# Weight decoding in three stages a unit apart, a split first load of P, and later loads kept behind, in a one-core kernel of packed attention and two mixtures

## The chip, the core and the metric

The kernel runs on one core of a Trainium2 chip, as one program with one launch. The metric is the device time in microseconds (us). The core has five engines that work in their own order: TensorE (PE, matrix products; PEld is its loading of weights), VectorE (DVE), ScalarE (ACT), GpSimd (POOL) and SyncE (SP), which here issues loads only. ScalarE and GpSimd issue a few as well.

## The reference

Batch B = 4, heads H = 8, sequence S = 576, head dimension D = 64, and 32 packed queries. Attention runs twice: the packed queries p over (k, v), and then q over what that gave. Its output is 2304 tokens of width 512, which go through two layers with 2048 hidden units and Mish, and then through another two with ELU.

```python
def sm_attn(qq, kk, vv):
    s = scale * np.matmul(qq, kk.transpose(0, 1, 3, 2))
    s = s - np.max(s, axis=-1, keepdims=True)
    a = np.exp(s)
    a = a / (np.sum(a, axis=-1, keepdims=True) + 1e-09)
    return np.matmul(a, vv)
p_packed = sm_attn(p, k, v)
out = sm_attn(q, p_packed, p_packed)
...
h = x @ w_in
sp = np.where(h > 20.0, h, np.log1p(np.exp(np.minimum(h, 20.0))))
g = h * np.tanh(sp)
y = g @ w_out
...
h = y @ w_in2
g = np.where(h > 0.0, h, alpha * (np.exp(np.minimum(h, 0.0)) - 1.0))
return g @ w_out2
```

q, k, v and p arrive as float32, the four weight matrices as float64.

## The kernel before, in words

**Weights.** Nothing on the chip computes in float64, so a weight tile of 128 x 512 numbers is loaded as 128 x 1024 integers (`load_raw`, L123) and put together into float32 by `decode` (L135): s0, a prelude on ScalarE (L158 in the form for the beginning, `exps`, with Prelu; L160 with Copy after it); s1 to s3, the merge, on VectorE (L165, L173, L178; the `exps` form has no L173); s4, the high half, on ScalarE (L200); s5, the low half, on VectorE (L206). Products are made in three terms, high by high, high by low and low by high. The tiles of the first layer of mixture 1 (w1i) are not split but kept whole in w1v, and GpSimd stores them in DRAM, from where they are loaded again for later batches (w1r).

**Attention and fold.** `attention_steps(b)` gives the steps of one batch: k is turned (kT), scores of P over k (L302), maximum, exponential and sum (L316 to L333), turning, the packed product (L373, L403), whose result is copied to PT (L271); then q is turned, the second scores (L426 for batch 0, L441 for the others) are turned to tokens by rows (L455), and after exponential and norm they come back as A2h and A2l, two halves (L204). `fold(b, c)` multiplies PT into a quarter of w1i (L519) and splits the result into G[b, c]. So the first layer of mixture 1 is one product of G with A2.

**Units.** Mixture 1 runs over 128 units: four batches, two halves of tokens, 16 blocks of 128 hidden units. A unit is `gemm1` (6 products, L550 to L552, first of them the term high by high), `mish` (Mish on ScalarE L559, high half on ScalarE L560, low half on VectorE L561) and, two units later (LAG), `gemm2` (12 products, L578 to L580, which add to an output in PSUM). In batch 0 the order is blocks 0 to 7 for the first half of the tokens, the same for the second, and then 8 to 15. Mixture 2 (L640 to L665) follows with the same kind of loop; its weights are decoded during mixture 1.

**What sets the order.** `startup()` is written out by hand: on TensorE, VectorE, ScalarE and SyncE its instructions are pinned in the order of the list `order`, in which `parts(n, 1, 3)` stands for steps 1 and 3 of the n-th tile. Eight tiles are decoded there. After it, `mixture1` is a loop over units, and the framework's scheduler may move instructions past each other, apart from those that `tc.keep_in_program_order` names: the prelude and the first merging step of a tile. In the loop, `DEC1=[9, 37]` tells how many w1 tiles are to be decoded by which unit; `decode_w1(m)` runs all six steps of a tile one behind the other. Folds 1 to 3 of batch 0 start at the units in `F0`. Batch 1's attention goes one step at a time, and from unit `FAST0` on at a second place of each unit too.

**Loads.** SyncE issues its loads in one order. An issue that would be the ninth under way waits for one that was issued eight places earlier (ScalarE's issues count among these). A raw tile of mixture 1 lies in a buffer of the pool `up`, and its load also waits until the buffer's last user is done.

Of the kernel before, what the change touches and what calls it, by code (L numbers as in the profile page):

```python
# [9 lines left out]
F32 = mybir.dt.float32  # L10
F32R = mybir.dt.float32r
# [7 lines left out]
    DEC1=[9, 37],  # L19
    F0=[3, 12, 17],  # L20
    LEAD=2,
    ATT1=4,
    FAST0=16,
# [18 lines left out]
def kernel(  # L42
# [71 lines left out]
    pT = const.tile([128, B * H // 2, 2, NP], F32, name="pT")  # L114
# [8 lines left out]
    def load_raw(name, r, c):  # L123
        nm = f"raw_{name}{r}_{c}"
        t = slot([128, 1024], I32, nm) if name[1] == "1" else sg.tile([128, 1024], I32, tag="sg", name=nm)
        nc.sync.dma_start(
            out=t, in_=weights[name][r * 128:(r + 1) * 128, c * 1024:(c + 1) * 1024]
        )
        raws[name, r, c] = t
# [5 lines left out]
    def decode(name, r, c, staged=False, exps=False):  # L135
# [3 lines left out]
        t = dp.tile([128, 512], I32, tag="dec", name="dec")  # L139
# [12 lines left out]
        oi = w1v[key][:, r % 2, :].bitcast(I32) if whole else t  # L152
# [29 lines left out]
        def s4():  # L182
            if whole:
                if r % 2 == 1:
                    nc.gpsimd.dma_start(out=w1_dr[c * 2 + r // 2], in_=w1v[key])
            else:
                split_hi(t.bitcast(F32), parts[:, 0] if staged else wt[key][0][:, r % 2, :], 1.0 / WSCALE)
# [103 lines left out]
    def scores1(b, s):  # L291
        d = {}

        def pe():
            ps = pm()
            d["pair"] = last_pair[0]
            for x in range(2):
                for g in (3, 2, 1, 0):
                    kg = kT[b, g].rearrange("p e s -> p (e s)").rearrange("p (j x t) -> p j x t", x=2, t=32)
                    for th in range(2):  # L300
# [3 lines left out]
                            lhsT=pT[r:r + 32, b * 4 + g, x, :],  # L304
# [206 lines left out]
    def fold(b, c):  # L511
# [20 lines left out]
        return [pe, post]  # L532
# [205 lines left out]
    def decode_w1(m):  # L738
        for _ in range(m):
            if w1dec:  # L740
                for f in next_w1():
                    f()

# [4 lines left out]
    DEC1 = P["DEC1"]  # L748

    def startup():  # L750
        pr = slot([128, B * H // 2, D], F32, "pr")
        ps_ = p.rearrange("b (g s) n d -> s n (b g) d", s=2)
        for s in range(2):
            for th in range(2):
                r = 64 * s + 32 * th
                (nc.sync, nc.scalar)[s].dma_start(out=pr[r:r + 32], in_=ps_[s])
# [13 lines left out]
        load_w1(6)  # L770
# [10 lines left out]
        nc.vector.transpose(  # L781
            out=pT.rearrange("p g x k -> p (g x k)"), in_=pr.rearrange("p g d -> p (g d)")
        )
        a1t0, a1t1 = ta
        order = [
            hk[0][0], hk[1][0], hk[2][0], hk[3][0], sc[0][0], sc[1][0], *parts(0, 0), *parts(0, 1, 3, 4, 5),
            sc[0][1], *parts(1, 0), sc[1][1], *parts(1, 1, 3, 4, 5), sc[0][2], a1t0[0], a1t0[1], pk[0][0], a1t1[0], a1t1[1],
            hq[0][0], hq[1][0], sc[1][2], *parts(2, 0), *parts(3, 0), pk[0][1], pk[1][0], hq[2][0], hq[3][0], pk[1][1], pk[0][2],
            *parts(2, 1, 3), pk[1][2], s2[0], *parts(2, 4, 5), *parts(3, 1, 3, 4, 5), f0[0], s2[1], s2[2],
            s2[3], s2[4], *parts(4, 0), f0[1], s2[5], *parts(4, 1, 3), s2[6], *parts(4, 4), s2[7], *parts(4, 5),  # L790
            *parts(5, 0, 1, 3, 4, 5), *parts(6, 0, 1, 3, 4, 5), *parts(7, 0, 1, 3, 4, 5),
        ]
        for o in order:
            o()

# [17 lines left out]
    def mixture1():  # L813
# [28 lines left out]

        tile2 = 2 * (B - 1) * NK + P['T2']
        for c in (3, 2, 1):
            fol.q.appendleft((F0[c - 1], fold(0, c)))
        for i in range(NA + LAG):
# [101 lines left out]
```

## Time and profile before

| | |
|---|---|
| time, median of 3 runs | 829.34 us (828.67 to 830.78) |
| the profiled execution's own time | 830.86 us |
| its span | 829.1 us |
| mean granted TensorE clock | 0.96 |
| busy: TensorE, VectorE, ScalarE, GpSimd | 777.5, 440.1, 346.6, 22.6 us |
| moved by DMA | 96.80 MB |

The rows further down come from that one profiled execution, in microseconds from the start of its span. A timeline row is a run of like instructions of one line: start, length from the first to the last, engine, line, operation, what it writes and reads, how many, and in brackets the idle time of the engine before it and what ended it. The granted clock is a share of TensorE's full speed, 1.00 being 2.4 GHz and 0.50 being 1.2. Busy time is the time in which an engine worked on an instruction; TensorE's products overlap, so the start of one after another tells the pace, not the length of one.

### The profile page before, as it was taken

The numbers are of one execution on the slowest core, as the hardware profiler recorded it, in microseconds if no ns is written. First come the engines' busy times: TensorE is split into PE (matmuls) and PEld (weight loads), VectorE is DVE, ScalarE is ACT, GpSimd is POOL, SyncE is SP. The second block draws the span as 40 slices with busy tenths as digits, with TensorE's granted clock in tenths as the row PEclk, the third lists the DMA queues.
The fourth block names the chain that finished last, engine by engine and source line by source line (L and its number), as shares of the span: only waits on it lengthen the run. The fifth ranks groups of instructions, "written<-read, shape, count | busy, mean of one in ns | idle before, by whom it ended". The sixth has DMA issues, their size and how long they took to land.

```text
span 829.1 us, 13056 instructions
## 1 busy us (share of the span) xinstructions
PE 777.5 (94%) x5212; PEld 671.0 (81%) x5212; DVE 440.1 (53%) x844; ACT 346.6 (42%) x676; POOL 22.6 (3%) x46
## 2 busy tenths in 40 slices
PE   3656898999999999999999999999999999999997
PEld 3344788979989898899998888888888888888886
DVE  3678788675587466772516753513253334342342
ACT  1265774557465655674534432312141223221222
POOL 0000000000101000000000000000000000000000
PEclk7565998999999999999999999999999999999999
DMA  9954377237656656431592310200020001000000
GB/s 273 372 215 158 120 272 220 81 111 222 197 198 244 191 142 233 142 116 51 180 332 79 127 52 26 76 1 1 1 76 14 1 0 51 13 0 1 26 26 26
DMA packets 69181, 96.80 MB, mean 117 GB/s; under 512 B 36096, under 2 KB 44800, under 8 KB 69120
## 3 DMA queue, kind: packets, MB, share of 16 engines
q1 hardware_dynamic: 62176, 77.22, 29.6%
q0 software_dynamic: 4736, 17.30, 5.3%
q10 hardware_dynamic: 2208, 1.44, 0.7%
q8 instruction: 41, 0.67, 0.3%
q14 instruction: 20, 0.16, 0.1%
HBM read 73.92 MB, written 22.02 MB: 116 GB/s over the span
## 4 chain that ended last, share of the span: by engine, by line
PE 85%; DVE 6%; ACT 4%; DMA 3%; issue 1%; SPq 0%; ACTq 0%; DVEq 0%
PE h L640 8%; PE h L641 8%; PE h L642 8%; PE o L663 8%; PE o L664 8%; PE o L665 8%; PE acc L579 7%; PE acc L578 7%; PE acc L580 7%; PE h L550 4%; PE h L551 4%; PE h L552 4%; PE pm L519 1%; DMA raw_w1i<-in_moe_w_in_dram 1%; DMA raw_w2i<-in_moe_w_in_dram 1%
## 5 line engine op out<-in xcount | busy, mean ns | idle before, releaser
L578 PE MATMUL acc<-gh,w1oh 128*128 128x288 f32 x512 | 150.1, 300 | 5.6 <-ACT w1oh L200 3.4
L579 PE MATMUL acc<-gl,w1oh 128*128 128x288 f32 x512 | 152.8, 300 | 0.1
L580 PE MATMUL acc<-gh,w1ol 128*128 128x288 f32 x512 | 152.3, 300 | 0.0
L641 PE MATMUL h<-yl,w2ih 128*128 128x512 f32 (+1 forms) x320 | 117.7, 368 | 0.0
L642 PE MATMUL h<-yh,w2il 128*128 128x512 f32 (+1 forms) x320 | 117.5, 368 | 0.0
L640 PE MATMUL h<-yh,w2ih 128*128 128x512 f32 (+1 forms) x320 | 116.7, 368 | 0.0
L663 PE MATMUL o<-w2oh,gh 128*128 128x512 f32 x288 | 112.4, 390 | 1.1 <-ACT ob L269 0.7
L664 PE MATMUL o<-w2ol,gh 128*128 128x512 f32 x288 | 112.2, 390 | 0.0
L644 ACT ACTIVATE t<-h 128x512 f32<-128x512 f32 (+1 forms) x80 | 42.8, 553 | 165.3 <-PE h L642 157.5
L665 PE MATMUL o<-w2oh,gl 128*128 128x512 f32 x288 | 108.3, 389 | 0.0
L645 DVE TENSOR_SCALAR t<-t 128x512 f32<-128x512 f32 (+1 forms) x80 | 31.7, 399 | 142.3 <-ACT t L644 141.5
L578 PEld LDWEIGHTS acc<-gh,w1oh 128*128 128x128 f32 x512 | 96.9, 192 | 10.1 <-ACT w1oh L200 3.8
L579 PEld LDWEIGHTS acc<-gl,w1oh 128*128 128x128 f32 x512 | 97.7, 191 | 6.5 <-DVE gl L561 3.2
L580 PEld LDWEIGHTS acc<-gh,w1ol 128*128 128x128 f32 x512 | 97.5, 191 | 5.0 <-issue 4.5
L561 DVE TENSOR_TENSOR gl<-t,gh 128x288 fp32r<-128x288 f32 x128 | 57.8, 453 | 77.9 <-ACT gh L560 77.3
L550 PE MATMUL h<-a2h,gh 128*128 128x288 f32 x256 | 78.7, 310 | 14.4 <-ACT a2h L200 10.5
L559 ACT ACTIVATE t<-h 128x288 f32<-128x288 f32 x128 | 52.2, 409 | 81.4 <-PE h L552 80.1
L551 PE MATMUL h<-a2l,gh 128*128 128x288 f32 x256 | 77.8, 304 | 2.9 <-DVE a2l L204 2.9
L200 ACT ACTIVATE gh<-t 128x512 fp32r<-128x512 f32 (+1 forms) x80 | 46.6, 588 | 78.6 <-DVE t L646 49.5
L552 PE MATMUL h<-a2h,gl 128*128 128x288 f32 x256 | 77.1, 303 | 0.0
L204 DVE TENSOR_TENSOR gl<-t,gh 128x512 fp32r<-128x512 f32 (+1 forms) x80 | 50.3, 638 | 41.0 <-ACT gh L200 39.5
L642 PEld LDWEIGHTS h<-yh,w2il 128*128 128x128 f32 x320 | 60.3, 188 | 10.3
(107 smaller groups left out, 1101.5 us busy)
## 6 DMA issues: line engine op xcount, KB each, us to landing
w1r<-w_dr SPq DMA_DIRECT2D x24, 512.0 KB, 6.4
raw_w2i<-in_moe_w_in_dram SPq DMA_DIRECT2D x16, 512.0 KB, 4.4
raw_w1i<-in_moe_w_in_dram SPq DMA_DIRECT2D x16, 512.0 KB, 8.1
raw_w1o<-in_moe_w_out_dram SPq DMA_DIRECT2D x16, 512.0 KB, 8.1
raw_w2o<-in_moe_w_out_dram SPq DMA_DIRECT2D x16, 512.0 KB, 3.7
k<-in_k_dram SPq DMA_DIRECT2D x16, 288.0 KB, 4.6
y_dr<-y POOLq DMA_DIRECT2D x16, 288.0 KB, 2.9
w_dr<-w1v POOLq DMA_DIRECT2D x8, 512.0 KB, 5.1
```

Source lines behind the costliest of these rows:

```text
L550: nc.tensor.matmul(out=hp, lhsT=wh, rhs=xh, start=(kt == 0), stop=False)
L551: nc.tensor.matmul(out=hp, lhsT=wh, rhs=xl, start=False, stop=False)
L552: nc.tensor.matmul(out=hp, lhsT=wl, rhs=xh, start=False, stop=(kt == 1))
L578: nc.tensor.matmul(out=o, lhsT=wh[:, cs], rhs=gh, start=first, stop=False)
L579: nc.tensor.matmul(out=o, lhsT=wh[:, cs], rhs=gl, start=False, stop=False)
L580: nc.tensor.matmul(out=o, lhsT=wl[:, cs], rhs=gh, start=False, stop=last)
L640: nc.tensor.matmul(out=hp, lhsT=wh, rhs=xh, start=(i == 0), stop=False)
L641: nc.tensor.matmul(out=hp, lhsT=wh, rhs=xl, start=False, stop=False)
L642: nc.tensor.matmul(out=hp, lhsT=wl, rhs=xh, start=False, stop=(i == 3))
L663: nc.tensor.matmul(out=o, lhsT=gh[:, ts], rhs=wh, start=(kk == 0), stop=False)
L664: nc.tensor.matmul(out=o, lhsT=gh[:, ts], rhs=wl, start=False, stop=False)
L665: nc.tensor.matmul(out=o, lhsT=gl[:, ts], rhs=wh, start=False, stop=(kk == NK - 1))
```

## The change

- Decoding in stages. In the loop of mixture 1, each unit starts one tile (unit 0: two): load of the next one, and its prelude (s0). Tiles so started stand in `staged`. Of these, each unit merges (s1 to s3) as many as `NDEC=[2, 4, 6]` and then one more per unit ask for, ahead of `gemm1`; the halves (s4, s5) follow behind `mish` of the next unit. `decode_w1` is gone.
- The merge of a w1i tile writes at once into w1v, without the buffer `dec`.
- P is loaded in two pieces: batch 0 (a quarter) as before by SyncE and ScalarE, the other three by GpSimd's queue ahead of the identity matrix; they are turned at the end of `startup` (`turn_p(1)`).
- The raw loads of mixture 2's weights are kept in program order (`keep_in_program_order`), so the scheduler no longer moves them forward.
- `startup`: ten tiles have their prelude in it and six are finished in it (before: eight and eight); the steps of the tiles stand at other places among those of attention; low halves of G[0, 0] are a step of their own (`post_lo`). Two more tiles are asked for ahead.
- `F0` goes from units 3, 12, 17 to 3, 13, 19, and `FAST0` from 16 to 24.

```diff
-    DEC1=[9, 37],
-    F0=[3, 12, 17],
+    NDEC=[2, 4, 6],
+    F0=[3, 13, 19],
...
-    FAST0=16,
+    FAST0=24,
...
-        nc.sync.dma_start(
+        ins = nc.sync.dma_start(
             out=t, in_=weights[name][r * 128:(r + 1) * 128, c * 1024:(c + 1) * 1024]
         )
+        if name[1] == "2":
+            tc.keep_in_program_order(ins)
...
-        oi = w1v[key][:, r % 2, :].bitcast(I32) if whole else t
+        wv = w1v.get(key)
+        oi = wv[:, r % 2, :].bitcast(I32) if whole else dp.tile([128, 512], I32, tag="dec", name="dec")
+        t = oi
...
-        return [pe, post]
+        return [pe, post] if b or c else [pe, post_hi, post_lo]
...
+        pr = [slot([128, n * H // 2, D], F32, f"pr{n}") for n in (1, B - 1)]
...
+                    eng = nc.gpsimd if x else (nc.sync, nc.scalar)[s]
+                    eng.dma_start(out=pr[x][r:r + 32], in_=ps_[s][:, a:a + n, :])
...
-        load_w1(6)
+        load_w1(8)
...
-        dec = [decode(*w1dec.popleft(), exps=True) for _ in range(8)]
+        dec = [decode(*w1dec.popleft(), exps=True) for _ in range(10)]
...
-            hk[0][0], hk[1][0], hk[2][0], hk[3][0], sc[0][0], sc[1][0], *parts(0, 0), *parts(0, 1, 3, 4, 5),
...
+            hk[0][0], hk[1][0], hk[2][0], hk[3][0], sc[0][0], sc[1][0], sc[0][1], sc[1][1], *parts(0, 0), sc[0][2],
+            a1t0[0], a1t0[1], a1t1[0], a1t1[1], *parts(1, 0), pk[0][0], hq[0][0], hq[1][0], sc[1][2], *parts(0, 1, 3, 4),
+            pk[1][0], pk[0][1], hq[2][0], hq[3][0], pk[0][2], pk[1][1], *parts(2, 0), *parts(3, 0), *parts(1, 1, 3, 4),
+            pk[1][2], s2[0], *parts(2, 1, 3, 4), *parts(3, 1, 3, 4), s2[1], s2[2], f0[0], s2[3], s2[4], f0[1],
+            *parts(4, 0), *parts(5, 0), s2[5], f0[2], *parts(6, 0), *parts(7, 0), s2[6], s2[7],
+            *parts(8, 0), *parts(9, 0), *parts(4, 1, 3, 4), *parts(5, 1, 3, 4), *parts(4, 5), *parts(5, 5),
+            lambda: turn_p(1),
         ]
...
+        staged.extend(dec[6:])
...
-            if len(w1seq) - len(w1dec) < DEC1[0] + (i + 1) * DEC1[1] // 32:
-                m = DEC1[0] + (i + 1) * DEC1[1] // 32 - (len(w1seq) - len(w1dec))
-                load_w1(m + LEAD - (len(w1dec) - len(w1load)))
-                decode_w1(m)
+
+            now = []
+            if staged:
+                done = P["NDEC"]
+                n = done[i] if i < len(done) else done[-1] + i + 1 - len(done)
+                while staged and nmerged[0] < n:
+                    now.append(staged.popleft())
+                    nmerged[0] += 1
+            for _ in range(2 if i < 1 else 1):
+                if w1dec:
+                    load_w1(1)
+                    staged.append(next_w1())
+                    staged[-1][0]()
+            for t in now:
+                for f in t[1:4]:
+                    f()
             if i < NA:
                 gemm1(i)
             if i < NA:
                 mish(i)
+            for t in merged:
+                for f in t[4:6]:
+                    f()
+            merged[:] = now
```

How the instructions stand on the engines shows more than the diff, since the scheduler moves some of them. In the rows below a line is one instruction in its engine's order, L is the line of the kernel (lines of the changed kernel lie 1 to 15 further down), and the numbers behind a name tell buffers apart. First SyncE, from the last k of batch 0 on. Before:

```order
L249 DMA k0_3_148<-in_k_dram 128x576
L126 DMA raw_w2i0_1_1924<-in_moe2_w_in_dram 128x1024
L126 DMA raw_w2i1_1_1926<-in_moe2_w_in_dram 128x1024
L126 DMA raw_w1i0_0_163<-in_moe_w_in_dram 128x1024
L126 DMA raw_w1i1_0_165<-in_moe_w_in_dram 128x1024
L249 DMA q0_0_167<-in_q_dram 128x576
L249 DMA q0_1_169<-in_q_dram 128x576
```

After the change:

```order
L253 DMA k0_3_154<-in_k_dram 128x576
L127 DMA raw_w1i0_0_169<-in_moe_w_in_dram 128x1024
L127 DMA raw_w1i1_0_171<-in_moe_w_in_dram 128x1024
L253 DMA q0_0_173<-in_q_dram 128x576
L253 DMA q0_1_175<-in_q_dram 128x576
L253 DMA q0_2_177<-in_q_dram 128x576
L253 DMA q0_3_179<-in_q_dram 128x576
```

The two loads of raw_w2i, mixture 2's weights, are no longer there: the first tiles of mixture 1 (raw_w1i) and q follow k at once.

Second, VectorE right behind the turning of k. Before:

```order
L281 STREAM_TRANSPOSE kT0_3_212<-k0_3_148 128x576
L165 TENSOR_SCALAR dec_191<-raw_w1i0_0_163 128x512
L178 SCALAR_TENSOR_TENSOR w1v0_0_192<-raw_w1i0_0_163,dec_191 128x512
L316 TENSOR_REDUCE sm_251<-pm_214 128x1
L317 TENSOR_SCALAR sm_251<-sm_251 128x1
L316 TENSOR_REDUCE sm_258<-pm_231 128x1
L317 TENSOR_SCALAR sm_258<-sm_258 128x1
L165 TENSOR_SCALAR dec_193<-raw_w1i1_0_165 128x512
L178 SCALAR_TENSOR_TENSOR w1v0_0_192<-raw_w1i1_0_165,dec_193 128x512
```

After the change:

```order
L285 STREAM_TRANSPOSE kT0_3_219<-k0_3_154 128x576
L320 TENSOR_REDUCE sm_255<-pm_221 128x1
L321 TENSOR_SCALAR sm_255<-sm_255 128x1
L320 TENSOR_REDUCE sm_261<-pm_238 128x1
L321 TENSOR_SCALAR sm_261<-sm_261 128x1
L337 TENSOR_SCALAR rs_268<-sm_255 128x1
L340 RECIPROCAL rs_268<-rs_268 128x1
L275 COPY a1t0_0_277<-pm_271 128x512
L275 COPY a1t0_0_277<-pm_271 64x128
```

The merging of the first two tiles (L165, L178) has left the place ahead of the maxima (L316, now L320) and between them and what follows (L337 ff.).

Third, ScalarE in the first units of mixture 1; t and gh are Mish and its high half, w1oh is the high half of a tile of the second layer, raw_w1o and raw_w1i are preludes. Before, from unit 2 on:

```order
L559 ACTIVATE t1_534<-h1_527 128x288
L200 ACTIVATE w1oh0_0_198<-dec_200 128x512
L158 ACT_TABLE_LOAD
L158 ACTIVATE raw_w1o2_0_183<-raw_w1o2_0_183 128x512
L560 ACTIVATE gh1_535<-t1_534 128x288
L559 ACT_TABLE_LOAD
L559 ACTIVATE t1_585<-h1_578 128x288
L560 ACTIVATE gh1_586<-t1_585 128x288
L200 ACTIVATE w1oh2_0_202<-dec_201 128x512
```

After the change, from the first Mish on:

```order
L572 ACT_TABLE_LOAD
L572 ACTIVATE t1_485<-h1_478 128x288
L204 ACTIVATE w1oh0_0_203<-dec_205 128x512
L573 ACTIVATE gh1_486<-t1_485 128x288
L572 ACTIVATE t1_512<-h1_505 128x288
L573 ACTIVATE gh1_513<-t1_512 128x288
L572 ACTIVATE t1_539<-h1_532 128x288
L204 ACTIVATE w1oh0_0_203<-dec_206 128x512
L164 ACTIVATE raw_w1i2_1_197<-raw_w1i2_1_197 128x512
```

The preludes of the next tiles and two table loads for them stood between Mish and its high half; the preludes now follow in the form that needs no table load, and a tile's high half stands in another unit than its prelude.

Elsewhere: GpSimd has the four loads of P's later batches between clearing the identity matrix and filling it. On SyncE k of batch 1 stands behind two more raw_w1i. On TensorE 48 products of the second layer stand between batch 1's packing and the first products of unit 20, where it was 30; 52 of them and two folds stand between batch 1's second scores (L445, before L441) and the first products of unit 32. On VectorE the two last transposes of batch 1's q stand ahead of the last low half of G[0, 3], and the turning of P's later batches stands at the end of the beginning.

## Rows read from the trace of the kernel before

**Rows 1.** Page of the profile: busy us (share of the span) xinstructions of each engine.

```profile
PE 777.5 (94%) x5212; PEld 671.0 (81%) x5212; DVE 440.1 (53%) x844; ACT 346.6 (42%) x676; POOL 22.6 (3%) x46
```

**Rows 2.** Busy time of each engine by stretches; then granted clock, DMA share, GB/s.

```profile
50.15:71.96 21.81, 13.58 (x70) 12.12 (x71) 17.19 (x32) 15.28 (x25) 0.53 (x1) 0.73 0.22 68
...
50.90:133.40 82.50, 65.56 (x536) 55.78 (x535) 66.64 (x133) 55.58 (x106) 3.42 (x6) 0.83 0.53 171
...
160.00:180.00 20.00, 19.43 (x164) 15.88 (x164) 18.72 (x37) 13.38 (x27) 1.61 (x3) 1.00 0.15 49
180.00:824.00 644.00, 643.30 (x4016) 559.76 (x4015) 307.21 (x584) 254.09 (x496) 14.52 (x27) 1.00 0.29 93
```

**Rows 3.** Timeline of SyncE, 0 to 24 us: start, length, DMA issues of one line.

```profile
3.67 1.27 SPq L126 DMA_DIRECT2D raw_w2i<-in_moe_w_in_dram  x2
10.66 2.81 SPq L126 DMA_DIRECT2D raw_w1i<-in_moe_w_in_dram  x2
```

**Rows 4.** Waits of SyncE's DMA queue, 0 to 24 us: total, times, longest.

```profile
SPq L126 <- DMA raw_w2i<-in_moe_w_in_dram: 5.7, 1, 5.7
```

**Rows 5.** DMA issues from 3.1 to 3.6, from 15.3 to 16 us: to landing.

```profile
k<-in_k_dram SPq DMA_DIRECT2D x2, 288.0 KB, 4.8
...
q<-in_q_dram SPq DMA_DIRECT2D x2, 288.0 KB, 7.3
```

**Rows 6.** Timeline, 0 to 95 us: start, length, work, idle before and what ended it.

```profile
9.24 1.95 PE L302 MATMUL pm<-kT,pT 32*32 32x288 f32 x64 [2.49 <-DVE kT L281]
...
20.06 0.53 ACT L321 ACTIVATE e<-pm,sm 128x320 f32<-128x320 f32 x1 [2.14 <-DVE sm L317]
...
25.79 1.43 DVE L281 STREAM_TRANSPOSE qT<-q 128x576 f32<-128x576 f32 x2
...
31.39 0.43 DVE L271 COPY pt<-pm 64x256 f32<-64x256 f32 x1
...
34.53 1.58 DVE L455 STREAM_TRANSPOSE x<-pm 128x288 f32<-128x288 f32 x4 [1.53 <-PE pm L426]
...
40.82 0.69 DVE L206 SCALAR_TENSOR_TENSOR gl<-pm,gh 128x512 fp32r<-128x512 f32 x1 [1.83 <-ACT gh L200]
...
45.57 0.39 DVE L165 TENSOR_SCALAR dec<-raw_w1o 128x512 int32<-128x512 int32 x1
...
45.99 0.69 DVE L178 SCALAR_TENSOR_TENSOR dec<-raw_w1o,dec 128x512 int32<-128x512 int32 x1
...
50.15 0.61 PE L551 MATMUL h<-a2l,gh 128*128 128x288 f32 x1 [2.89 <-DVE a2l L204]
```

**Rows 7.** Waits of VectorE, 50.9 to 133.4 us: total, times, longest.

```profile
DVE gl L561 <- ACT gh L560: 3.4, 4, 1.1
...
DVE w1ol L206 <- ACT w1oh L200: 3.1, 4, 1.0
DVE gl L206 <- ACT gh L200: 1.3, 2, 0.7
DVE dec L165 <- ACT raw_w1o L158: 1.3, 1, 1.3
DVE dec L165 <- DMA raw_w1i<-in_moe_w_in_dram: 1.3, 1, 1.3
```

**Rows 8.** Timeline of TensorE, 57 to 135 us: the second fold of batch 0.

```profile
71.96 1.96 PE L519 MATMUL pm<-w1v,pt 64*32 64x512 f32 x16 [4.73 <-DVE w1v L178]
```

**Rows 9.** Timelines around batch 1's second scores and the fold after them.

```profile
155.24 0.29 PE L578 MATMUL acc<-gh,w1oh 128*128 128x288 f32 x1
155.37 0.29 PE L579 MATMUL acc<-gl,w1oh 128*128 128x288 f32 x1
155.59 0.72 PE L441 MATMUL pm<-qT,pt 64*32 64x288 f32 x16
...
167.60 0.75 DVE L204 TENSOR_TENSOR a2l<-a2t,a2h 128x576 fp32r<-128x576 f32 x1
...
168.15 1.09 PE L519 MATMUL pm<-w1r,pt 64*32 64x512 f32 x16
```

More of the change, by code (lines that the diff above doesn't have):

```diff
@@ L113 @@
     ident = const.tile([128, 128], F32, name="ident")
-    pT = const.tile([128, B * H // 2, 2, NP], F32, name="pT")
+    pT = [const.tile([128, n * H // 2, 2, NP], F32, name=f"pT{n}") for n in (1, B - 1)]
     y_dr = [dr.tile([128, 4, HALF], F32, name=f"y_dr{i}") for i in range(2 * B)]
@@ L138, in decode @@
         w0, w1 = rr[:, :, 0], rr[:, :, 1]
-        t = dp.tile([128, 512], I32, tag="dec", name="dec")
         f1 = w1.bitcast(F32)
@@ L184, in s4 @@
                 if r % 2 == 1:
-                    nc.gpsimd.dma_start(out=w1_dr[c * 2 + r // 2], in_=w1v[key])
+                    nc.gpsimd.dma_start(out=w1_dr[c * 2 + r // 2], in_=wv)
             else:
@@ L303, in pe @@
                             out=ps[th][32 * g:32 * g + 32, 0:HALF],
-                            lhsT=pT[r:r + 32, b * 4 + g, x, :],
+                            lhsT=pT[b > 0][r:r + 32, max(b - 1, 0) * 4 + g, x, :],
                             rhs=kg[r:r + 32, :, x, :],
@@ L530, in post, with post_hi, post_lo @@
                 split(d["ps"][s], G[b, c][0][:, s, :], G[b, c][1][:, s, :], 1.0 / WSCALE)
-        return [pe, post]
+        def post_hi():
+            G[b, c] = [slot([128, 2, 512], F32R, f"g{x}{b}_{c}") for x in "hl"]
+            for s in range(2):
+                split_hi(d["ps"][s], G[b, c][0][:, s, :], 1.0 / WSCALE)
+        def post_lo():
+            for s in range(2):
+                split_lo(d["ps"][s], G[b, c][0][:, s, :], G[b, c][1][:, s, :], 1.0 / WSCALE)
+        return [pe, post] if b or c else [pe, post_hi, post_lo]
     gt1, ht = {}, {}
@@ L736, in next_w1 @@
         return decode(*w1dec.popleft())
[L738 to L742, printed above, removed]
     WARM = P["WARM"]
@@ L747 @@
     F0 = P["F0"]
-    DEC1 = P["DEC1"]
+    staged = deque()
     def startup():
-        pr = slot([128, B * H // 2, D], F32, "pr")
+        pr = [slot([128, n * H // 2, D], F32, f"pr{n}") for n in (1, B - 1)]
         ps_ = p.rearrange("b (g s) n d -> s n (b g) d", s=2)
[L753 to L756, printed above, removed]
+        for x, (a, n) in enumerate(((0, H // 2), (H // 2, (B - 1) * H // 2))):
+            for s in range(2):
+                for th in range(2):
+                    r = 64 * s + 32 * th
+                    eng = nc.gpsimd if x else (nc.sync, nc.scalar)[s]
+                    eng.dma_start(out=pr[x][r:r + 32], in_=ps_[s][:, a:a + n, :])
         make_identity(nc, ident)
@@ L775, in startup, with turn_p @@
         f0 = fold(0, 0)
-        dec = [decode(*w1dec.popleft(), exps=True) for _ in range(8)]
+        dec = [decode(*w1dec.popleft(), exps=True) for _ in range(10)]
         def parts(n, *which):
             return [dec[n][i] for i in which]
-        nc.vector.transpose(
-            out=pT.rearrange("p g x k -> p (g x k)"), in_=pr.rearrange("p g d -> p (g d)")
-        )
+        def turn_p(x):
+            nc.vector.transpose(
+                out=pT[x].rearrange("p g x k -> p (g x k)"), in_=pr[x].rearrange("p g d -> p (g d)")
+            )
+        turn_p(0)
         a1t0, a1t1 = ta
         order = [
-            hk[0][0], hk[1][0], hk[2][0], hk[3][0], sc[0][0], sc[1][0], *parts(0, 0), *parts(0, 1, 3, 4, 5),
[L787 to L791, printed above, removed]
+            hk[0][0], hk[1][0], hk[2][0], hk[3][0], sc[0][0], sc[1][0], sc[0][1], sc[1][1], *parts(0, 0), sc[0][2],
[5 more added lines that the diff above has]
+            lambda: turn_p(1),
         ]
@@ L841, in step_w2 @@
                 cur.popleft()()
+        nmerged, merged = [0], []
         tile2 = 2 * (B - 1) * NK + P['T2']
```

## Prediction

> **What bounds the kernel now.** I read the busy shares on the page first [rows 1]: TensorE is busy 777.5 of 829.1 us, so 51.6 us are idle. A table by stretches says where [rows 2]: from 180 to 824 us it is busy 643.3 of 644.0, so nothing is to be had there; in 50.15 to 71.96 us it is busy 13.58 of 21.81, at a mean granted clock of 0.73. All but a few of the idle microseconds lie in the first 135, where the change works.
>
> Next I followed the beginning, along the loads. SyncE issues two tiles of the second mixture, raw_w2i, from 3.67 us, and the first tile of the first mixture only at 10.66 [rows 3]; that issue stood 5.7 us waiting for raw_w2i to land [rows 4]. So 1 MB that nobody needs for 100 us goes ahead of the first weights and of q. The last k, issued at 3.2, lands 4.8 us later, at 8.0; the last q, issued at 15.6, lands 7.3 us later, at 22.9 [rows 5].
>
> Then the timeline of VectorE [rows 6]. The scores are done at 11.2 us, but the first exponential starts at 20.06: its maximum stood in VectorE's order behind the decoding of a weight tile that had to land first. The two halves of PT are copied by 31.82, the second scores are turned from 34.53, and TensorE has its first full-length product (L551) at 50.15, after 2.89 us of waiting for a2l.
>
> After that VectorE, not TensorE, sets the pace of batch 0. From 50.90 to 133.40 it is busy 66.64 of 82.50 us [rows 2], and its waits are of one kind: prelude on ScalarE, merge on VectorE, high half on ScalarE, low half on VectorE, one tile's four steps back to back [rows 7]. At 135.0 the 21st unit (unit 20) begins; from there TensorE hardly stops.
>
> **The change, part by part.** The sum runs against the profiled execution: 830.86 us, of which 829.1 are the span. It lies 1.5 us above the median of the three runs, which I take off at the end.
>
> *A, the beginning.* With the second mixture's loads pinned behind, the first w1i is issued when the last k lands, 8.0 instead of 10.66, and the queue is 1 MB shorter: the last q lands at about 20.0 instead of 22.9 (2.7 from the earlier issue, and a little from the shorter queue). The reductions and exponentials no longer stand behind a decoded tile, so both halves of the packing are done before q is there, and q becomes what is late. From 20.0: the last two transposes of q 1.43 [rows 6]; then PT's two copies (0.43 each), one tile's two merging steps (0.39 and 0.69) and a small scaling that I put at 0.3 give 2.2, so 23.6. From the last PT copy to the turning of the scores took 2.7 (31.82 to 34.53) and is unchanged: 26.4, against 34.53, or 8.1 us earlier. In the next stretch, 34.53 to 50.15, VectorE loses the 1.83 us wait for G's high half, since the normalizing now stands before it, and the two merging steps of w1o's first tile, 1.1: 2.9 more. **A = -11.0.** Bounds: at least -6 (q lands when it did, and of the second part only the tile's steps go); at most -15 (q is not late either: the exponential starts at 11.4, right after its scores, instead of 20.06, which is 8.7; the merging of the three tiles that stand before the turning, 1.1 each, falls into VectorE's waits, 3.3; and the 2.9).
>
> P's first batch is now a quarter as large and lands sooner, but k is later anyway: nothing. P's other batches are issued by GpSimd before it finishes the identity, so the warm-up products shift by some 2 to 3 us; the scores wait for k, and q is late behind both: nothing. If that cover were gone, the shift itself is the price.
>
> *B, the decoding a unit apart.* Low halves, high halves and merges of one tile now stand in different units, and more tiles have their prelude before the first Mish table is loaded. Of VectorE's 15.9 us idle I expect the waits for w1oh (3.1), for G's high half (1.3), for a prelude (1.3) and for the late raw_w1i (1.3) to go: -7.0 [rows 7]. Those for mish's high half (3.4) and the rest, of other kinds, stay. Against this, work enters the stretch: the rest of P, 768 columns at q's 0.72 for 576, 0.95; the two merging steps of w1o's first tile, 1.1; two transposes of q that now stand ahead of G's last low half, 1.4; and out goes one step of 0.69 for each of two more tiles of the short kind, 1.4. Together +2.1. **B = -4.9.** Bounds: +2 (the waits only move) and -13 (all idle goes). I stay near the middle because half of the waits have a partner that the change doesn't touch. Raw tiles now stay in their buffers a unit longer; SyncE's loads wait for such buffers, but from 50.15 to 71.96 the DMA engines were busy for a 0.22 share only [rows 2], so that costs nothing until loads get late (rival four).
>
> *C, work done ahead.* Before unit 20's products TensorE now has 48 second-layer products behind the last packing, where it had 30. 18 at 0.13 us, the distance from one product's start to the next [rows 9], are **-2.4**; at worst 0.
>
> *D, batch 1's attention comes later.* FAST0 goes from 16 to 24, so its second scores end nearer to unit 32, which needs them. That chain (turn, maximum, exponential, sum, transpose, split) ran from 156.31, where the scores end, to 168.35, where the last split does: 12.0 us [rows 9]. TensorE had enough to do meanwhile; in the new order 52 products (0.13 each) and two folds (1.09 each) stand between, 9.0 us. **D = +3.0**, from 0 to +9 if VectorE is behind as well.
>
> *Clock.* A fold took 1.96 us at 71.96, right after 4.73 us of idle [rows 8], and 1.09 at 168.15 [rows 9], where the clock is at 1.00 [rows 2]. While VectorE sets the pace a slower TensorE costs nothing, so I take 0, and the other end as a rival.
>
> Sum: -11.0 - 4.9 - 2.4 + 3.0 = -15.3; 830.86 - 15.3 - 1.5 = **814 us**.
>
> **The rivals.** *One, the waits only move* (the stages fill ScalarE's queue instead): B loses its 7.0, and 821 remains. For it: ScalarE works in order, and its high halves stand among Mish. Against it: ScalarE was only 55.6 of 82.5 us busy in the stretch [rows 2].
>
> *Two, the beginning gives all of it*: A = -15 and D hidden, 807. For it: scores were done 8 us before anybody looked at them. Against it: q needed 7.3 us where k needed 4.8 [rows 5], so the queue in front of it is what makes it late, and most of that queue stays.
>
> *Three, slower: the clock.* Between units TensorE will pause for VectorE all through the stage. If it is then granted 1.2 instead of 2.4 GHz throughout, it becomes the bound itself: 360 products at 0.13 and 11 us of folds and attention are 58 us at full clock, and at 1.96/1.09 times that 104 us; from 39.2 that ends at 143, against 135 now, and with C and D the whole takes 838. It decides from the point where four fifths of this work run at the lower level. In 50.15 to 71.96 us a mean of 0.73 means 54% of the time [rows 2], so it isn't far away; but the slow fold followed a block of 4.73 us of idle [rows 8], and the change makes the pauses shorter. The Trainium skill (TensorE: Matmul & The Clock Gate, Part 1) says it the other way round, that the low clock is the default and sustained activity releases it. By that rule many short pauses are as bad as one long one, and this rival gets its chance; the trace, with 0.73 in a stretch that was busy for 62%, does not contradict it.
>
> *Four, no change: loads are the bound.* If the decoding can't run ahead because the tiles don't land ahead (k of batch 1 now stands behind two more of them, and in VectorE's queue ahead of the decoding), only the 2.7 us of the earlier issue remain and D takes them: about 829. Against it: the 0.22 share again [rows 2].
>
> **How the numbers follow.** A measurement of this kernel tells 0.3%, 2.5 us, from no change. Forecast 0.58, rival one 0.14, two 0.14, three 0.08, four 0.06. Faster is forecast, one and two, 0.86; same 0.06; slower 0.08. The ends of A, B and D seldom meet: two thirds of the way to each good bound gives about 804, to each bad one about 825. That takes in rivals one and two and leaves out three, four and the tails, some 2 in 10.
>
> **What would show it.** A: raw_w1i is issued near 8 us, the first exponential starts before 14, the scores are turned near 26 and L551 starts near 39. B: VectorE's waits for w1oh and for preludes are gone from the stage, and unit 20 begins near 117 (135 less A, B and C). D: a pause of about 3 us before batch 1's first products. It is wrong if L551 starts after 45, if VectorE idles 12 us or more between a2l and unit 20, or if the clock before unit 20 is below 0.7.

## The result, and the profile after

The changed kernel takes 820.68 us (median of 4 runs, 819.11 to 822.85) against 829.82 us before; the ratio is 0.9892, with a 95% interval of 0.9866 to 0.9919. So it is 9.1 us faster, where 15.3 were forecast. One execution of e7 below ran slow (976.66 us at a granted clock of 0.743, where all others have 0.958 or more) and stands neither in its median nor in its ratio.

A word on lines: all of them moved. L551 before, the first product that needs a2l, is L564 now; the halves L200 and L206 are L204 and L210, the merge L165 and L178 is L169 and L182, Mish's low half L561 is L574. First the page: busy times, and the granted clock in 40 slices.

```profile
PE 780.3 (95%) x5212; PEld 673.1 (82%) x5212; DVE 437.2 (53%) x843; ACT 342.8 (42%) x674; POOL 25.0 (3%) x50
...
PEclk9579989899999999999999999999999999999999
```

TensorE is busy 780.3 us where it was 777.5 [rows 1], in a span that is 10.1 shorter: idle fell from 51.6 to 38.7, by 12.9, and 2.8 of that went into longer busy time.

To see where, I counted TensorE's products in both timelines and took the times at which units 20, 32 and 40 have their first product, with the number of second-layer products that stand before it. "First a2l" is the start of L551 or its counterpart.

| profiled execution | first a2l | unit 20 (products before) | unit 32 (before) | unit 40 (before) | span |
|---|---|---|---|---|---|
| before | 50.15 | 134.99 (222) | 167.79 (374) | 190.92 (456) | 829.1 |
| changed | 39.58 | 114.13 (240) | 155.60 (384) | 178.81 (456) | 819.0 |
| difference | -10.6 | -20.9 | -12.2 | -12.1 | -10.1 |

Unit 20 comes 20.9 us earlier, with 18 products more behind it, which are worth another 2.3 (at 0.13 each): 23.2 us ahead. At unit 40, with equal work done on both sides, 12.1 are left, and 10.1 at the end. More was won than I forecast, and 13 us of it were given back, nearly all between units 20 and 40. The stretches of the changed kernel show the same (columns as in [rows 2]).

```profile
0.00:39.58 39.58, 20.44 (x279) 13.79 (x280) 26.47 (x52) 12.38 (x26) 4.48 (x12) 0.76 0.98 335
39.58:114.13 74.55, 66.89 (x564) 58.33 (x564) 63.99 (x131) 47.90 (x101) 3.20 (x6) 0.90 0.75 246
114.13:155.60 41.47, 36.38 (x299) 30.49 (x297) 28.88 (x58) 18.81 (x39) 1.09 (x2) 0.96 0.23 69
155.60:178.81 23.21, 22.20 (x168) 19.23 (x169) 13.76 (x28) 12.79 (x27) 1.62 (x3) 0.85 0.80 261
178.81:400.00 221.19, 220.19 (x1923) 201.69 (x1922) 138.79 (x276) 131.91 (x272) 13.50 (x25) 1.00 0.50 159
```

From 39.58 to 114.13 VectorE is busy 63.99 of 74.55 us and the clock is 0.90 in the mean; before it was 66.64 of 82.50 and 0.83 in the nearly equal stretch of [rows 2]. The next two rows are where it goes: TensorE is busy only 36.38 of 41.47 us and 22.20 of 23.21, the second at a clock of 0.85. Before, TensorE hardly idled once unit 20 had begun; the same four stretches there, from the first a2l on:

```profile
50.15:134.99 84.84, 67.89 (x545) 58.12 (x546) 68.92 (x136) 56.78 (x109) 3.42 (x6) 0.83 0.54 172
134.99:167.79 32.80, 32.72 (x274) 30.24 (x273) 23.51 (x49) 18.07 (x36) 1.09 (x2) 1.00 0.37 128
167.79:190.92 23.13, 22.64 (x213) 18.35 (x211) 17.75 (x33) 12.35 (x27) 1.64 (x4) 1.00 0.46 167
190.92:412.11 221.19, 221.19 (x1939) 203.56 (x1938) 136.92 (x276) 130.18 (x273) 13.42 (x25) 1.00 0.54 169
```

The beginning, from four engines' timelines; it answers to [rows 3] and [rows 6].

```profile
10.77 0.80 SPq L127 DMA_DIRECT2D raw_w1i<-in_moe_w_in_dram  x2
...
10.78 0.78 DVE L285 STREAM_TRANSPOSE kT<-k 128x576 f32<-128x576 f32 x1 [1.40 <-DMA k<-in_k_dram]
...
21.29 1.43 DVE L285 STREAM_TRANSPOSE qT<-q 128x576 f32<-128x576 f32 x2
...
27.70 1.58 DVE L459 STREAM_TRANSPOSE x<-pm 128x288 f32<-128x288 f32 x4 [0.46 <-PE pm L430]
...
13.96 0.53 ACT L325 ACTIVATE e<-pm,sm 128x320 f32<-128x320 f32 x1 [0.82 <-DVE sm L321]
...
39.58 0.61 PE L564 MATMUL h<-a2l,gh 128*128 128x288 f32 x1 [3.03 <-DVE a2l L208]
```

The chain of work that ended last (start, length) ran in this beginning over a load of raw_w2i and the first of raw_w1i before the change:

```profile
3.67 6.98 DMA raw_w2i<-in_moe_w_in_dram
10.66 6.58 DMA raw_w1i<-in_moe_w_in_dram
```

After it, it runs over a load of v and the first of q:

```profile
4.07 7.77 DMA v<-in_v_dram
...
11.85 6.41 DMA q<-in_q_dram
```

From 18.27, where that load of q lands, the chain goes on almost wholly on VectorE and TensorE.

The waits of VectorE in the stage (total, times, longest), which answer to [rows 7]:

```profile
DVE gl L210 <- ACT gh L204: 2.6, 3, 2.0
DVE gl L574 <- ACT gh L573: 1.9, 2, 1.3
DVE pv L390 <- PE pm L377: 1.8, 1, 1.8
DVE w1ol L210 <- ACT w1oh L204: 0.4, 1, 0.4
```

The wait for w1oh is 0.4 us instead of 3.1, and none for a prelude or a raw tile is left among them. That for G's high half (L210, gl) grew from 1.3 to 2.6. Two more waits of the kernel before, from the same stretch as [rows 7], belong beside these; the first of them has no counterpart after the change:

```profile
DVE rs L333 <- ACT e L321: 3.2, 2, 1.9
...
DVE qT L281 <- DMA q<-in_q_dram: 0.6, 1, 0.6
```

The timelines of SyncE and VectorE at unit 20 show what replaced them:

```profile
104.50 10.52 SPq L262 DMA_DIRECT2D q<-in_q_dram  x8
...
110.50 0.46 DVE L574 TENSOR_TENSOR gl<-t,gh 128x288 fp32r<-128x288 f32 x1
115.49 0.78 DVE L285 STREAM_TRANSPOSE qT<-q 128x576 f32<-128x576 f32 x1 [4.54 <-DMA q<-in_q_dram]
116.30 0.69 DVE L210 SCALAR_TENSOR_TENSOR gl<-pm,gh 128x512 fp32r<-128x512 f32 x1
116.91 0.78 DVE L285 STREAM_TRANSPOSE qT<-q 128x576 f32<-128x576 f32 x1
117.61 0.65 DVE L210 SCALAR_TENSOR_TENSOR w1ol<-dec,w1oh 128x512 fp32r<-128x512 f32 x1
118.18 0.68 DVE L210 SCALAR_TENSOR_TENSOR gl<-pm,gh 128x512 fp32r<-128x512 f32 x1
```

SyncE issues the last eight of q's loads (two tiles) from 104.50 to 115.02, and VectorE stands 4.54 us for the first of the two. Behind that transpose, in its order, are the two low halves of G[0, 3] (L210, gl), and units 20 to 23 need those. What TensorE waited for from 100 to 165 us:

```profile
PE h L565 <- DVE gl L210: 2.7, 2, 2.2
PE h L563 <- ACT a2h L204: 2.3, 1, 2.3
...
PE h L564 <- DVE a2l L208: 0.9, 1, 0.9
```

2.7 us for these low halves, and 2.3 and 0.9 for batch 1's a2h and a2l before unit 32.

### The profile page after: what moved, and what is told of

Same layout as the page of the kernel before. It is cut to its first block, busy times and chain, and to the rows that moved or that the text cites. A ratio compares the mean times of both kernels' runs of the same rounds, so it can differ in the third digit from the quotient of the medians.

```text
span 819.0 us, 13054 instructions
## 1 busy us (share of the span) xinstructions
PE 780.3 (95%) x5212; PEld 673.1 (82%) x5212; DVE 437.2 (53%) x843; ACT 342.8 (42%) x674; POOL 25.0 (3%) x50
## 4 chain that ended last, share of the span: by engine, by line
PE 77%; issue 7%; DVE 6%; DMA 5%; ACT 3%; SPq 1%; POOL 0%; ACTq 0%; POOLq 0%; DVEq 0%
PE h L654 8%; PE h L653 8%; PE h L655 8%; PE o L676 8%; PE o L677 8%; PE o L678 8%; PE acc L593 6%; PE acc L591 6%; PE acc L592 6%; PE h L563 3%; PE h L564 3%; PE h L565 3%; DMA q<-in_q_dram 2%; PE pm L523 1%; DMA v<-in_v_dram 1%
## 5 line engine op out<-in xcount | busy, mean ns | idle before, releaser
L574 DVE TENSOR_TENSOR gl<-t,gh 128x288 fp32r<-128x288 f32 x128 | 57.9, 453 | 77.7 <-ACT gh L573 77.1
L564 PE MATMUL h<-a2l,gh 128*128 128x288 f32 x256 | 78.4, 307 | 3.9 <-DVE a2l L208 3.9
L204 ACT ACTIVATE gh<-t 128x512 fp32r<-128x512 f32 (+1 forms) x80 | 46.6, 588 | 78.8 <-DVE t L659 49.2
L653 PEld LDWEIGHTS h<-yh,w2ih 128*128 128x128 f32 x320 | 60.3, 188 | 10.3
```

Source lines behind the costliest of these rows:

```text
L564: nc.tensor.matmul(out=hp, lhsT=wh, rhs=xl, start=False, stop=False)
L653: nc.tensor.matmul(out=hp, lhsT=wh, rhs=xh, start=(i == 0), stop=False)
```

## The experiments

Twelve kernels, each timed in five rounds beside the kernel before on the same chip. The ratio is to that kernel. A thousandth is 0.83 us.

| run | median us | ratio, 95% interval | first a2l | unit 20 | unit 40 |
|---|---|---|---|---|---|
| e5 changed kernel again | 821.22 | 0.9883 (0.9867 to 0.9899) | 40.39 | 113.54 | 179.87 |
| e1 loads free | 825.13 | 0.9933 (0.9920 to 0.9945) | 41.16 | 115.63 | 180.91 |
| e2 whole tiles | 825.76 | 0.9943 (0.9932 to 0.9955) | 41.13 | 126.71 | 185.88 |
| e3 FAST0 = 20 | 815.87 | 0.9832 (0.9817 to 0.9848) | 39.76 | 112.97 | 173.77 |
| e4 q behind | 815.64 | 0.9823 (0.9810 to 0.9835) | 41.03 | 115.57 | 174.28 |
| e6 P late | 821.05 | 0.9876 (0.9857 to 0.9895) | 40.74 | 117.28 | 181.91 |
| e7 P in front | 823.58 | 0.9909 (0.9893 to 0.9926) | 41.55 | 115.95 | 181.16 |
| e8 both | 810.85 | 0.9764 (0.9751 to 0.9778) | 40.11 | 114.69 | 168.86 |
| e9 v behind k | 821.65 | 0.9896 (0.9882 to 0.9909) | 40.13 | 113.43 | 180.22 |
| e10 both, whole tiles | 821.82 | 0.9896 (0.9881 to 0.9911) | 40.20 | 126.14 | 184.56 |
| e11 before, pinned | 828.30 | 0.9977 (0.9968 to 0.9987) | 47.76 | 132.15 | 188.48 |
| e12 early high half | 813.63 | 0.9804 (0.9789 to 0.9820) | 41.05 | 118.30 | 172.47 |

My theory after reading the two traces: the beginning and the staging each brought about 10 us by unit 20, and two separate new waits, q's late load in VectorE's order and batch 1's late attention, took most of the rest back. The main rival: staging only puts VectorE's work off, and what is put off has to be paid later in any case.

**e5, the changed kernel again.** No edit.

> The changed kernel once more, unaltered, so that the next three stand beside it on one chip. Every theory: 820.7 within 1.5 us, ratio to the kernel before 0.989 within 0.002.

821.22, ratio 0.9883. The first a2l is 0.8 us later than in the other profile of the same kernel, so up to a microsecond there says nothing.

### The two waits after unit 20

**e3.**

```diff
-    FAST0=24,
+    FAST0=20,
```

> The changed kernel with FAST0 = 20 instead of 24: batch 1's second scores come earlier, its folds later. Theory (TensorE's 3.2 us idle before unit 32, waiting for a2h and a2l, come from batch 1's attention being late): that idle goes, and the time is 2 to 3 us below 820.7, so 818. Rival (VectorE is what is late there, or the wait comes back at the folds): the wait moves to the split of a fold, and the time stays within 1 us of 820.7.

5 thousandths below e5, some 4 us. TensorE's waits from 100 to 165 us:

```profile
PE h L565 <- DVE gl L210: 3.8, 1, 3.8
...
PE h L564 <- DVE a2l L208: 0.9, 1, 0.9
```

The 2.3 us for a2h are gone, and from 152.69 to 173.77 (unit 32 to 40) the clock is 1.00 in this run, where the changed kernel has 0.85 in its stretch from unit 32 to 40:

```profile
152.69:173.77 21.08, 19.99 (x171) 16.52 (x170) 16.20 (x31) 12.05 (x27) 1.61 (x3) 1.00 0.59 207
```

The 0.9 for a2l and the wait for the low halves of G[0, 3] stay, the latter even longer, at 3.8.

**e4.** The fold's low halves and two transposes of q are pinned, and the attention steps with the transposes start later:

```diff
-                att.q.append((a0, s))
+                att.q.append((max(a0, 20) if b == 1 and n >= 12 else a0, s))
...
+            if nm[0] == "q" and b == 1 and g >= 2:
+                tc.keep_in_program_order(ins)
...
+            pin[0] = (b, c) == (0, 3)
```

> The changed kernel with two transposes of batch 1's q put behind the low halves of the fold before unit 20 (G[0, 3]) in VectorE's order. Theory (VectorE stood 4.5 us waiting for the load of q with that low half behind it, and so cost TensorE 2.7 us of idle and some time at the lower clock): that idle goes and the time is 2 to 4 us below 820.7, so about 817.5. Rival (what is gained at unit 20 is given back as a longer wait for a2h before unit 32, which VectorE's chain sets): unit 22 starts 3 us earlier, unit 32's products do not, and the time stays within 1 us of 820.7.

6 thousandths below e5, 5 us. In TensorE's waits from 100 to 165 us the low halves no longer appear; the first row is now

```profile
PE h L571 <- ACT a2h L206: 2.3, 1, 2.3
```

that is, the wait before unit 32 stands unchanged at 2.3. Behind it the clock is 0.85 here too, with TensorE busy almost throughout:

```profile
151.89:174.28 22.39, 22.37 (x169) 18.64 (x169) 13.78 (x28) 12.83 (x27) 1.62 (x3) 0.85 0.83 272
```

So neither wait covers for the other, and the rival, that the gain is given back before unit 32, falls.

**e8.** Both edits.

> Both single edits that gained 5 us: FAST0 = 20 and the two transposes of q behind the low halves of G[0, 3]. Theory (two separate waits, one before unit 22 and one before unit 32): the gains add for the larger part, TensorE idles under 1 us at both places, and the time is 3 to 5 us below either, 811 to 813. Rival (both take away the same thing, VectorE's being late in units 20 to 32): 815 to 816, as either alone.

0.9764, 11.9 thousandths below e5, or 9.9 us; the single edits gave 4.2 and 5.0. They add. The stretches from unit 20 to 32 and on to 40:

```profile
114.69:147.11 32.42, 31.98 (x267) 29.26 (x265) 25.32 (x52) 18.07 (x36) 1.09 (x2) 1.00 0.30 91
147.11:168.86 21.75, 20.00 (x171) 16.54 (x169) 16.85 (x32) 12.02 (x27) 1.62 (x3) 1.00 0.52 188
```

TensorE is busy 31.98 of 32.42 us at full clock, where the changed kernel had 36.38 of 41.47. In the second stretch 1.75 us of idle are left, 1.5 of them for a2l. This version beats both kernels: 19.6 us below the one before.

### What the staging is worth

**e2.** The beginning stays, with eight tiles finished in it; the loop decodes whole tiles at the old pace:

```diff
+            if len(w1seq) - len(w1dec) - len(staged) < DEC1[0] + (i + 1) * DEC1[1] // 32:
...
+                for _ in range(m):
+                    if staged:
+                        for f in staged.popleft()[1:]:
+                            f()
```

> The changed kernel with its beginning, but in mixture 1's loop each tile is decoded whole again, all steps one behind the other, at the old pace (9 + 37/32 per unit), eight tiles finished in the beginning. Theory (staging the decoding a unit apart brings what the loop gained): L564 stays near 39.6, VectorE's waits for w1oh come back (3 us), unit 20 begins 7 to 13 us later, and the time is 825 to 828, since some of that was given back later anyway. Rival (the beginning is the whole gain): 820.7 within 1.5 us.

6 thousandths above e5, 5.0 us; unit 20 is 13.2 us later than in e5, of which 0.7 lie in the beginning. The staging gains over 12 us by unit 20, and the changed kernel kept 5 of them.

**e10.** The same in the version of e8.

> The run with both edits (FAST0 = 20, q behind the low halves; 810.9 us), but with each tile decoded whole in the loop, at the old pace. Theory (staging is worth 11 us at unit 20 and the two waits gave part of it back): without the two waits it is worth more than the 4.5 us that it was worth in the changed kernel, 7 to 11 us, so this run takes 818 to 822. Rival (what staging gains is given back further on in any case, VectorE having the same work to do): 5 us or less, 814 to 816.

0.9896, 13.2 thousandths above e8: 11.0 us, all of what the staging gains up to unit 20 (126.14 against 114.69). In the two profiles the distance is 15.7 at unit 40 and 13.4 at the end, but e10's profiled execution is the longest of its four, 2.7 above the median. VectorE's waits from 41 to 126 us show the old pattern again:

```profile
DVE dec L169 <- ACT raw_w1o L164: 4.0, 4, 1.6
...
DVE w1ol L212 <- ACT w1oh L206: 2.6, 5, 0.7
```

So the rival that VectorE pays later anyway falls: without the two waits, the staging keeps its gain to the end. It also says that the two edits help a kernel more that comes early to unit 20: with whole tiles they are worth 4.7 thousandths (0.9943 to 0.9896), with staging 11.9.

**e12.** More of the same idea on e8: the first waits for w1oh, at 52 us.

```diff
-    NDEC=[2, 4, 6],
+    NDEC=[2, 2, 6],
...
-            lambda: turn_p(1),
...
+            if i == 2:
+                late_p()
```

> The run with both edits (810.9 us), and two more moves on VectorE in units 0 to 2: P's later batches are turned in unit 2 instead of at the end of the beginning, and the merging of the first tiles for fold 1 waits for unit 2 (NDEC = 2, 2, 6), so that the two tiles of the second layer that units 2 and 3 wait for come 2 to 3 us sooner. Theory (one short wait there, 2.3 us for w1oh and 1.6 for w1ol, is paid twice, since TensorE's clock is granted at 0.5 to 0.75 in the 6 us behind it): the waits fall to under 1 us, the clock in 52 to 58 us is above 0.8, and the time is 2 to 4 us below 810.9, 807 to 809. Rival (VectorE has the same work up to fold 1, which then waits for w1v): the idle moves to fold 1 at 58 us, and the time stays within 1 us of 810.9.

A miss: 813.63, 4 thousandths above e8. In 52 to 58 and 58 to 66 us e8 has

```profile
52.00:58.00 6.00, 4.38 (x21) 4.15 (x22) 5.90 (x11) 1.19 (x2) 0.53 (x1) 0.74 0.74 238
58.00:66.00 8.00, 6.50 (x73) 4.03 (x72) 5.72 (x11) 4.11 (x9) 0.53 (x1) 0.98 0.87 275
```

and this run

```profile
52.00:58.00 6.00, 2.90 (x20) 2.67 (x20) 5.86 (x11) 0.50 (x1) 0.53 (x1) 1.00 0.57 197
58.00:66.00 8.00, 4.84 (x27) 3.03 (x28) 4.79 (x10) 2.73 (x5) 0.53 (x1) 0.51 0.89 301
```

with these waits of TensorE from 40 to 70 us:

```profile
PE pm L529 <- DVE w1v L182: 5.0, 1, 5.0
...
PE acc L601 <- DVE w1ol L212: 1.4, 1, 1.4
```

The wait for w1oh is gone, and fold 1 waits 5.0 us for w1v instead. From 58 to 66 us, the stretch in which that wait ends, the clock is 0.51. VectorE has no idle time there to give (busy 5.90 and 5.86 of 6.00 us), so what is drawn forward for one consumer is late for the next.

### The beginning

**e1.** The pins are taken from mixture 2's loads:

```diff
-        if name[1] == "2":
-            tc.keep_in_program_order(ins)
```

> The changed kernel with one part undone: mixture 2's first loads are no longer kept in program order. Theory (the order of the loads is part of the beginning's gain): raw_w2i is issued in front of raw_w1i again, the first raw_w1i at 13 us or later instead of 10.8, the first L564-type product (high by low, first of unit 0) 2 to 3 us later than 39.6, and the time 2 to 3 us longer than the changed kernel's 820.7, so about 823. Rival (the beginning waits for k and its own chain on VectorE, and the loads are hidden): L564 stays within 0.5 us of 39.6 and the time within 1 us of 820.7.

5 thousandths above e5, 4.2 us, more than the theory's 3. The first raw_w1i is issued at 12.06, and unit 20 comes 2.1 us later than in e5. But the first a2l, at 41.16, is no later than in some kernels with the pins, and the span, 821.1, is only 1.0 above e5's 820.1: the profiled execution is one of this kernel's shortest. The times say that the pins pay; where all of the 4 us lies is not shown here.

**e11.** The pins alone, in the kernel before.

```diff
+        if name[1] == "2":
+            tc.keep_in_program_order(ins)
```

> The kernel before with mixture 2's first loads kept in program order, and nothing else of the change. Theory (in its beginning a decoded tile stands ahead of the first exponential, so an earlier raw_w1i carries through): raw_w1i is issued at 8 to 9 instead of 10.66, the first exponential starts 2 us earlier than 20.06, L551 1.5 to 2.5 us earlier than 50.15, and the time is 2 to 3 us below the kernel before, ratio 0.997. Rival (q, behind k and v, lands no earlier and holds the chain): L551 within 0.5 us of 50.15 and the time the same within 1 us.

Ratio 0.9977, 1.9 us. The timelines of SyncE, ScalarE, VectorE and TensorE:

```profile
8.41 1.06 SPq L126 DMA_DIRECT2D raw_w1i<-in_moe_w_in_dram  x2
...
17.68 0.53 ACT L323 ACTIVATE e<-pm,sm 128x320 f32<-128x320 f32 x1 [2.14 <-DVE sm L319]
...
32.14 1.57 DVE L457 STREAM_TRANSPOSE x<-pm 128x288 f32<-128x288 f32 x4 [1.52 <-PE pm L428]
...
47.76 0.61 PE L553 MATMUL h<-a2l,gh 128*128 128x288 f32 x1 [2.89 <-DVE a2l L206]
```

Every step is 2.3 to 2.4 us earlier than its row in [rows 3] and [rows 6]: the issue (10.66), the exponential (20.06), the turning (34.53), the first a2l (50.15). The two loads that nobody needs yet cost nearly their whole delay at the front of the queue.

The next three look for why k's last part is turned at 10.78 in the changed kernel, when in the kernel before it landed at 8.0.

**e6.** P's later batches go to SyncE, behind q.

```diff
-                    eng = nc.gpsimd if x else (nc.sync, nc.scalar)[s]
...
+                nc.sync.dma_start(out=pr[1][r:r + 32], in_=ps_[s][:, H // 2:B * H // 2, :])
```

> The changed kernel with the three later batches of P issued by SyncE behind batch 0's q, in place of GpSimd's queue at the start. Theory (these four transfers compete with k, whose last part lands at 10.8 us instead of 8.0): the last k is turned near 8.5, the first raw_w1i is issued near 8.5, L564 starts at 37 to 38, and the time is 1.5 to 3 us below the changed kernel. Rival (k lands late for another reason, the loads of v beside it): k stays at 10.8 to 12, and the time is within 1 us of the changed kernel, or above it by what the four issues cost SyncE, 2 us.

**e7.** All of P goes in front, in its two pieces.

```diff
-                    eng = nc.gpsimd if x else (nc.sync, nc.scalar)[s]
+                    eng = (nc.sync, nc.scalar)[s]
```

> The changed kernel with all of P issued by SyncE and ScalarE ahead of k and v, as in the kernel before but in two pieces. Theory (it is GpSimd's queue beside k that makes k late, not the bytes): the last k is turned near 9, as in the kernel before (8.0), L564 starts at 38 to 39, and the time is 1 to 2 us below the changed kernel. Rival (the bytes ahead of k count the same wherever they are issued): k is turned at 10.8 to 12, and the time is within 1 us of the changed kernel.

**e9.** v goes behind k, on SyncE.

```diff
-            load_vt(0, kt, nc.scalar)
+            load_vt(0, kt, nc.sync)
```

> The changed kernel with batch 0's v issued by SyncE behind k, in place of ScalarE beside it. Theory (v, whose issues start 1.2 us earlier since ScalarE has less of P to issue, shares the DMA engines with k and is why k's last part lands at 10.8 us and not at 8.0): the last k is turned by 9, ScalarE's table is loaded before its scores are there, L564 starts 1 to 2 us earlier than 39.6 to 40.4, and the time is about 1.5 us below the changed kernel's 821. Rival (q is what is late, and v ahead of q makes it later): q's last part lands 2 us or more after 21, L564 starts later than 40.4, and the time is above 821.

The turning of k's last part, on VectorE's timelines of e6, e7 and e9 in this order:

```profile
10.17 0.78 DVE L285 STREAM_TRANSPOSE kT<-k 128x576 f32<-128x576 f32 x1 [2.00 <-DMA k<-in_k_dram]
```

```profile
10.23 0.78 DVE L285 STREAM_TRANSPOSE kT<-k 128x576 f32<-128x576 f32 x1 [0.62 <-DMA k<-in_k_dram]
```

```profile
11.03 0.78 DVE L285 STREAM_TRANSPOSE kT<-k 128x576 f32<-128x576 f32 x1 [1.64 <-DMA k<-in_k_dram]
```

10.2, 10.2 and 11.0 us: none of the three brings 8.0 back, and none is faster than e5 beyond its interval. So none of my three causes (GpSimd's transfers beside k, P's place in the queue, v beside k) explains it alone. That two of them do it together is not excluded: in e6 v still goes out beside k, from 2.67, in e9 P's later batches do, from 1.37, and in e7 k's issues end a microsecond later, at 4.55 against 3.50. Why k lands later is open. It also mattered little, as the next section says.

## Why the prediction was right, and where it was not

The time lies in the range, and the direction is right. It came by a gain larger than forecast (23.2 us by unit 20 with C counted, where A, B and C make 18.3) and a loss that I had for the larger part not priced (13.1 given back, where D has 3.0). That the two misses are of opposite sign is luck. The time is close to rival one's 821, but not by its mechanism: the waits did not move from VectorE to ScalarE's queue, they went.

**A, the beginning: right in size, in one step by luck.** -10.6 measured (-9.8 in the second profile), -11.0 forecast. The step that the first raw_w1i is issued at 8.0 failed: k landed late, and it was 10.77. That cost little, because q did not hang on it: q's loads went out from 11.85 instead of 13.72, behind v's landings, and v's issues had started at 2.66 instead of 3.90. So q's landing came close to the forecast by another way than forecast: the last q, of which I had said 20.0, was issued at 13.48 and took 7.0 us, and so landed at 20.5. That is luck too. From q's last transposes to the turning I had 6.4 us (20.0 to 26.4), and it took 6.4 (21.29 to 27.70); the transposes came 1.3 late, the larger part of it because a tile's merge and a small scaling stood ahead of them on VectorE. The stretch from the turning to the first a2l was to shrink by 2.9 and shrank by 3.7 (15.6 to 11.9). The first exponential starts at 13.96, "before 14". The chain hung on q, as forecast, but on the landing of its first part and VectorE's work from there on. Of the 10.6, the order of the loads alone brought 2.4 in the old order of the steps (e11); what each of the other moves brought no run separates.

**B, the staging: right in kind, mis-sized.** -4.9 forecast; unit 20 comes 20.9 earlier, 10.6 of it from the beginning, which leaves -10.3. VectorE's idle time between the first a2l and unit 20 fell by 5.3, from 15.9 to 10.6, of which 3.2 are already the new wait for q; -7.0 was forecast. That these are near each other is in part luck. Of the four waits that were to go, three went or nearly so (5.7 to 0.4), but that for G's high half doubled (1.3 to 2.6), and VectorE got a new one of 1.8 for the packed product (L377). Instead a wait for the exponential (L333, 3.2) went, which I had left to stay with "the rest, of other kinds"; it was the second largest, so my reading that the waits "are of one kind" was wrong too. The failed step of B is the work: I let 2.1 us enter the stretch, and instead 4.9 left it (68.9 to 64.0). L173's 22 runs became 19 of L177; the two low halves of G[0, 3], at 0.69 each, and one more transpose of q, which I had standing before unit 20, now come behind its first product, because q is late. So a part of B was not saved but put off, to the place where the next wait arose. That the staging itself is worth 11.0 us at the end of the kernel is shown by e10 and e8.

**C, work done ahead: right as to the count.** 240 products against 222, as read from the order; what they are worth at the end no run measures. But "unit 20 near 117" took C off there, where it cannot show: by A and B alone it was 119, and 114.13 was measured.

**D, batch 1's attention: right as to the pause, short on the price.** A pause of 3 us was forecast before its first products, and it is 3.2 (2.3 and 0.9). The chain itself was longer than the 12.0 us I took: from the end of the second scores at 145.01 to the last split's at 159.51 it took 14.5, with two low halves of a fold and four sums of y among VectorE's steps. Undoing it (e3) gains 4.2 us, not 3.0: from 155.60 on the clock is 0.85, where it was 1.00 before and is 1.00 in e3; e4, which keeps the 2.3, has 0.85 as well. So the pause is paid a second time.

**What had no term.** Two transposes of q stood "ahead of G's last low half" in my text, priced at 1.4 us as work. I never asked when their data lands. In the kernel before, VectorE waited 0.6 us for q, and the last two transposes came behind the low halves; here SyncE issues the last q until 115.02, and the wait of 4.54 us has TensorE's next units behind it. Putting them behind gains 5.0 us (e4). That is the step of the prediction that failed: a wait in an ordered queue was priced by the length of the instruction and not by the arrival of what it waits for.

**The rivals.** Three, the clock, did not decide: 0.90 in the stage, after 0.83. But each pause brought some of it: 0.85 behind unit 32, 0.51 in e12 from 58 to 66 us, where a wait of 5.0 us ends. Four, the loads as the bound, was right at one point only, q, and that point cost about half of the missing gain. Two fell: the beginning gave no more than A, and D was not hidden. The upper end of the range was added up a little short: two thirds of the way to the bad ends of A, B and D give 826, not 825, which changes nothing here.

Of the 13.1 us given back, e8 recovers 9.9. About 2 are lost after unit 40 in the changed kernel and in e8 alike; in the changed kernel TensorE idles 1.00 us from 178.81 to 400, where it had no idle before. The rest of those 2 us I have not explained. Staging alone, in the old beginning, was not tried.

## What to carry to other kernels

When a change reorders an engine's work, list the instructions in it that wait for a DMA, and what now stands behind them. Price such an instruction by when its data lands, not by how long it runs. And judge an edit that removes waits with the next waits removed too: the staging looked worth 5 us in e2 and was worth 11 in e10, and the two edits behind it were worth 4 in the one surrounding and 10 in the other.

## What I had not expected of the hardware

A short idle of TensorE can be followed by products at the lower of its two levels. In e12 the stretch in which the wait of 5.0 us ends, 58 to 66 us, has a mean granted clock of 0.51, and in the changed kernel and e4, where a wait of 2.3 us ends at unit 32, it is 0.85 from there to unit 40. In e3 and e8, without that wait, it is 1.00 up to unit 40, though 1.09 and 1.75 us of idle lie within. The Trainium skill (TensorE: Matmul & The Clock Gate, Part 1) has the low clock as the default that sustained activity releases; these rows agree. So a wait could cost more than its length: e3, which takes those 2.3 us away, is 4.2 us faster.

k's last part landed 4.8 us after its issue in the kernel before and over 7 in the changed one, where v's loads start 1.2 us earlier and P's later batches go beside k on GpSimd's queue. Moving P or v alone changed little (k was turned at 10.2 to 11.0 us).
